# Attention and two mixtures of experts on one core: another order for the splits of k, v and q, and for six small operations of the routing

## The chip, the cores and the metric

One core of a Trainium2 chip runs the whole program in one launch. The metric is the device time of one launch in microseconds, the median of three runs: 1168.48 us (1166.46 to 1169.12). Profiles are of one execution each, which the hardware profiler records; their times are told beside their own execution's time.

## What is computed

```python
scores = scale * np.matmul(q, k.transpose(0, 1, 3, 2))          # 4 batches, 8 heads, 576 rows, 64 wide
scores = np.where(block_i >= block_j, scores, -1000000000.0)     # blocks of 64, causal by block
attn = np.exp(scores - np.max(scores, axis=-1, keepdims=True))
attn = attn / (np.sum(attn, axis=-1, keepdims=True) + 1e-09)
x = np.matmul(attn, v)                                           # heads joined: 2304 rows of 512
...
logits = xc @ w_gate                                             # rows with x @ w_skip > 0; expert = argmax of 8
gate_w = probs[np.arange(len(xc)), e_idx]
x[do_compute] = xc + gate_w * (np.maximum(xc @ w1[e], 0) @ w2[e])
...
out += p[:, e:e + 1] * (np.maximum(x @ w1[e], 0.0) @ w2[e])      # second mixture: all 4 experts, every row
```

Everything is float32 and is multiplied in pairs of a high part (a cast) and a low part (the rest), three products to a matmul.

## The kernel before

The program has three stages: attention with the routing (0 to about 224 us of the profile), the first mixture, and the second mixture, which is most of the time. The change lies in the first stage.

**Units.** Attention runs over 8 units of 4 heads (a batch, half its heads), numbered 0 to 7. Each unit has row tiles 0 to 4, in the order 0, 1, 3, 2, 4 (unit 7 in another): tile 0 has 64 rows and needs 64 columns of keys, tile rt has 128 rows and 64 + 128 rt columns. Tiles 2, 3 and 4 go as two items of two heads each, so a unit has 8 items. For each item TensorE (PE) writes scores `s` to PSUM (L285), VectorE (DVE) takes the row maxima `m` (L294), and ScalarE (ACT) writes the exponentials `E` (L301): 64 wide for tile 0, 192 for tile 1, 448 for tile 3, 320 for tile 2, 576 for tile 4. Then `E` is transposed to `eT`. Tiles 1 and 3 are transposed on PE (L327), and ACT and DVE write the high and low part (L329, L330). Tiles 0, 2 and 4 are split first: ACT casts `E` to the high half of `HL` (L333), GpSimd (POOL) subtracts (L334, 64x256, 128x640 and 128x1152 elements for the three tiles), and SyncE's queue (SP) starts a DMA that transposes (L335). PE multiplies `eT` with v into `og` (L359 to L361), and DVE divides (`r`, `x`, L367 to L370).

**Buffers of E.** `E` has four buffers (`EB = 4`), taken in turn. The fifth item of a unit, the first half of tile 2, takes the buffer of tile 0's item, so ACT's first `E` of 320 columns in a unit can't start until tile 0's split has read it, and the last to read it is POOL's subtraction of 64x256.

**The split of the next unit.** While a unit is scored, the parts of the next one are made by `split_unit`, a generator whose order a string sets: one letter is a step's work, a dot ends a step, and the attention loop runs two steps (`SN = 2`) for each group of scores. J scales k (ACT, L211); K casts it (ACT, `kh`, L212); k subtracts (POOL, `kl`, L213); V casts v (DVE, `vh`, L207) and v subtracts (POOL, `vl`, L208); A and B cast the two halves of q (ACT, `QH`, L230), a and b subtract (POOL, `QL`, L233); X and x copy pieces of q's parts for tile 4 (POOL, `q4h`, `q4l`, L222). Units 1 to 7 use `SO`, unit 0 `S0`.

**The routing.** When five or four tiles of x are done (two or one at the end), `route` picks each row's expert and its place in the sorted buffer `XS`: DVE makes one-hot rows `oh`, PE adds up ranks in the PSUM tile `pre` (L457 to L460), DVE sums the exponentials (L462 to L466) and multiplies `pre` by `oh` (L469), and POOL scatters the rows by indirect DMA (L478). `counts` (L491 to L502) follows the last batch.

The order on each engine is the order in which the Python code issues the work. Instructions of one engine run in that order.

Of the kernel before, what the change touches and what calls it, by code (L numbers as in the profile page):

```python
# [12 lines left out]
ALU = mybir.AluOpType  # L13
# [39 lines left out]
class Kernel:  # L53
# [49 lines left out]
    PW = 2  # L103
    PM = 1
    HV = ((7, 0),)
    SO = "J..K..V.k...A.v.B.a.b..X.x"

    def __init__(self, tc, q, k, v, wr, w11, w12, w21, w22, dp, out):
        self.tc, self.nc = tc, tc.nc
# [84 lines left out]
    def split_unit(self, u):  # L194

        nc = self.nc
        qr, kr, vr = self.raws.pop(u)
        QH = self.qk.tile([128, 2, S], F32R, name="QH")
        QL = self.qk.tile([128, 2, S], F32R, name="QL")
        KH, KL = self.kh[u % 2], self.kl[u % 2]  # L200
        vh, vl = self.vh[u % 3], self.vl[u % 3]
        self.units[u] = (QH, QL, KH, KL, vh, vl)
        V = nc.vector
        what = {
            "Q": lambda: nc.scalar.copy(QH, qr),
            "q": lambda: (V if self.QV else nc.gpsimd).tensor_tensor(QL, qr, QH.bitcast(F32), ALU.subtract),
            "V": lambda: V.tensor_copy(vh[:, :, :, 0:D], vr),  # L207
            "v": lambda: (V if self.VV else nc.gpsimd).tensor_tensor(vl, vr, vh[:, :, :, 0:D], ALU.subtract),  # L208
        }
        if u:  # L210
            what["J"] = lambda: nc.scalar.mul(kr, kr, 0.125)  # L211
            what["K"] = lambda: nc.scalar.copy(KH, kr)  # L212
            what["k"] = lambda: nc.gpsimd.tensor_tensor(KL, kr, KH.bitcast(F32), ALU.subtract)  # L213
        else:
            for x, y, i in (("0", "2", slice(0, 1)), ("1", "3", slice(1, 2))):
                what[x] = lambda i=i: V.tensor_scalar(KH[:, i], kr[:, i], 0.125, None, ALU.mult)
                what[y] = lambda i=i: V.scalar_tensor_tensor(KL[:, i], kr[:, i], 0.125, KH[:, i].bitcast(F32),
                                                             ALU.mult, ALU.subtract)
        def last(x):
            for a in range(2):  # L220
                p = slice(64 * a, 64 * a + 64)
                nc.gpsimd.tensor_copy(self.q4[u % 2][x][p].rearrange("p (c a) s -> p a c s", a=2)[:, a], (QH, QL)[x][p, :, S - 128:S])  # L222

        what["X"], what["x"] = lambda: last(0), lambda: last(1)
        for x in self.SO if u else self.S0:
            if x == ".":
                yield
            elif x in "AB":
                i = "AB".index(x)
                nc.scalar.copy(QH[:, i], qr[:, i])  # L230
            elif x in "ab":
                i = "ab".index(x)
                (V if i and not u else nc.gpsimd).tensor_tensor(QL[:, i], qr[:, i], QH[:, i].bitcast(F32), ALU.subtract)  # L233
            else:
                what[x]()
# [190 lines left out]
    def route(self, g, i0, i1):  # L426

        nc = self.nc
        n = i1 - i0
        yield from self.rest(self.RD)  # L430

        ts = []
        for x in range(i0, i1):
            i = (x + 4) % 5 if g == 3 else x
            ts.append((9 * (g // 2) + (5 * (g % 2) + i if i < 4 else 4), x - i0))
        lg = self.lgs[g][:, i0:i1]
        tl = lambda k, dt=F32: self.sm2.tile([128, 5, k], dt, tag=f"rt{k}{dt}", bufs=6, name="rt")[:, 0:n]
        mx, ex, cand, sm, ix, on = tl(1), tl(8), tl(8), tl(1), tl(1), tl(1)
        oh = tl(9, BF16)
        iota = self.iota[:, 0:n]  # L440
        nc.vector.tensor_reduce(mx[:, :, 0], lg[:, :, 0:8], axis=AX.X, op=ALU.max)
        nc.vector.tensor_tensor(ex, lg[:, :, 0:8], mx.to_broadcast([128, n, 8]), ALU.subtract)

        nc.vector.scalar_tensor_tensor(cand, ex, 0.0, iota, ALU.is_ge, ALU.mult)
        nc.vector.tensor_reduce(ix[:, :, 0], cand, axis=AX.X, op=ALU.min)
        nc.vector.tensor_tensor(cand, iota, ix.to_broadcast([128, n, 8]), ALU.is_equal)
        nc.vector.tensor_scalar(on, lg[:, :, 8:9], 0.0, None, ALU.is_gt)
        nc.vector.tensor_scalar(oh[:, :, 8:9], lg[:, :, 8:9], 0.0, None, ALU.is_le)
        nc.vector.tensor_tensor(oh[:, :, 0:8], cand, on.to_broadcast([128, n, 8]), ALU.mult)
        nc.scalar.activation(ex, ex, AF.Exp)  # L450
        yield
        yield from self.rest(self.PD)

        pre = self.pt([128, n, 9], "pre")
        for i in range(n):
            for j in range(i):
                nc.tensor.matmul(pre[:, i], lhsT=self.ones, rhs=oh[:, j], start=(j == 0), stop=False)  # L457
            nc.tensor.matmul(pre[:, i], lhsT=self.tri, rhs=oh[:, i], start=(i == 0), stop=False)
            nc.tensor.matmul(pre[:, i], lhsT=self.ones, rhs=self.hist, start=False, stop=False)
            nc.tensor.matmul(pre[:, i], lhsT=self.ones, rhs=self.base, start=False, stop=True)  # L460
        yield
        nc.vector.tensor_reduce(sm[:, :, 0], ex, axis=AX.X, op=ALU.add)  # L462
        nc.vector.tensor_scalar(sm, sm, 1e-9, None, ALU.add)
        for t, i in ts:
            x = self.x_of(t)
            nc.vector.reciprocal(x[:, DM + 1:RW], sm[:, i])  # L466
            nc.gpsimd.tensor_copy(x[:, DM:DM + 1].bitcast(I32), self.tok[:, t:t + 1])
        junk = tl(9)
        nc.vector.tensor_tensor(junk, pre, oh, ALU.mult)  # L469
        nc.vector.tensor_reduce(sm[:, :, 0], junk, axis=AX.X, op=ALU.add)  # L470
        sl = self.sm2.tile([128, 5], I32, tag="sl", bufs=5, name="sl")
        nc.vector.tensor_copy(sl[:, 0:n], sm[:, :, 0])
        for i in range(n):
            nc.vector.tensor_tensor(self.hist, self.hist, oh[:, i], ALU.add)
        for t, i in ts:
            while self.hold:
                yield
            ins = nc.gpsimd.indirect_dma_start(out=self.XS, out_offset=bass.IndirectOffsetOnAxis(ap=sl[:, i:i + 1], axis=0),  # L478
                                               in_=self.x_of(t), in_offset=None, bounds_check=E1 * N - 1,
                                               oob_is_err=False)  # L480

            for o in self.scat:
                self.tc.declare_no_dep(ins.ins, o.ins, reason="rows apart")
            self.scat.append(ins)
            for _ in range(self.XD):
                yield
# [744 lines left out]
```

## Time and profile before

| | |
|---|---|
| median of 3 runs | 1168.48 us (1166.46 to 1169.12) |
| profiled execution, its own time | 1173.74 us |
| span of its instructions | 1172.1 us, 1.6 us less than its time |
| granted clock of PE, mean of the span | 0.972 |
| PE busy | 1097.0 us (94%), 7197 matmuls |
| DVE, ACT, POOL busy | 760.6 us (65%), 518.0 us (44%), 574.1 us (49%) |

Busy shares over the whole span say little of the stage of the change: the second mixture, where PE is hardly ever idle, weighs most in them. The granted clock is in parts of full speed: 1.00 is 2.4 GHz, 0.50 is 1.2 GHz.

### The profile page before, as it was taken

To read this page: it belongs to the slowest core of one execution; us is meant where nothing else is said; L and a number is where in the kernel's file an instruction comes from. 1 tells how busy PE (TensorE), PEld (TensorE's weight loads), DVE (VectorE), ACT (ScalarE), POOL (GpSimd) and SP (SyncE) were. 2 spreads that over 40 slices of the span, in tenths; PEclk is the share of its full clock that TensorE was granted. 3 is DMA by queue.
4 is the path that set the end of the run, shared out by engine and by line. 5 is a ranking of instruction groups with operands and counts; after the bars stand their busy time and mean duration, and the time that the engine had idled before them with its cause. 6 is when DMAs were issued, how large, how long until landed. Compare 5 with 4: busy or idle time off the path is not lost.

```text
span 1172.1 us, 19018 instructions
## 1 busy us (share of the span) xinstructions
PE 1097.0 (94%) x7197; PEld 950.9 (81%) x7197; DVE 760.6 (65%) x1214; ACT 518.0 (44%) x852; POOL 574.1 (49%) x581
## 2 busy tenths in 40 slices
PE   5898978689999699999999999999999999999998
PEld 4788877567787589898899888999888888888886
DVE  6778776687528764666666666666846667676665
ACT  6988865366527544323232333233453333233331
POOL 6988883100111355454444454545665555555551
PEclk8999989699999799999999999999999999999999
DMA  5998849599614610111111111111321111111101
GB/s 194 217 226 200 179 118 253 170 323 388 235 46 158 218 55 20 53 37 40 52 36 36 38 36 54 36 37 54 128 71 54 54 54 55 55 54 55 36 1 72
DMA packets 119054, 123.04 MB, mean 105 GB/s; under 512 B 63341, under 2 KB 79725, under 8 KB 118928
## 3 DMA queue, kind: packets, MB, share of 16 engines
q1 hardware_dynamic: 116208, 116.82, 34.7%
q0 software_dynamic: 2720, 4.64, 1.1%
q8 instruction: 67, 1.10, 0.4%
q14 instruction: 59, 0.48, 0.1%
HBM read 91.83 MB, written 19.43 MB: 95 GB/s over the span
## 4 chain that ended last, share of the span: by engine, by line
PE 62%; DVE 3%; POOL 1%; ACT 1%; issue 1%; DMA 0%; SPq 0%; POOLq 0%
PE yp L672 11%; PE yp L671 11%; PE yp L673 11%; PE hp L672 9%; PE hp L673 9%; PE hp L671 9%; DVE xsl L875 1%; PE yp L732 0%; PE hp L713 0%; DVE acc L1005 0%; DVE xdl L865 0%; POOL C L943 0%; DVE C L943 0%; ACT hh L950 0%; DVE xs L871 0%
## 5 line engine op out<-in xcount | busy, mean ns | idle before, releaser
L1005 DVE SCALAR_TENSOR_TENSOR acc<-yp,p,acc 128x512 f32<-128x512 f32 x270 | 199.1, 747 | 109.3 <-PE yp L673 109.3
L950 ACT ACTIVATE hh<-C 128x512 fp32r<-128x512 f32 (+2 forms) x98 | 81.8, 834 | 349.2 <-DVE C L943 303.8
L671 PE MATMUL yp<-vh,hh 128*128 128x512 f32 x576 | 225.6, 392 | 2.8 <-ACT hh L950 2.4
L672 PE MATMUL yp<-vl,hh 128*128 128x512 f32 x576 | 226.3, 393 | 1.0 <-POOL vl L920 1.0
L673 PE MATMUL yp<-vh,hl 128*128 128x512 f32 x576 | 225.5, 391 | 0.3 <-DVE hl L951 0.3
L951 DVE SCALAR_TENSOR_TENSOR hl<-C,hh 128x512 fp32r<-128x512 f32 (+2 forms) x98 | 93.7, 957 | 99.6 <-ACT hh L950 99.6
L943 POOL TENSOR_TENSOR p<-C,p 128x256 f32<-128x256 f32 (+2 forms) x49 | 50.4, 1029 | 199.6 <-ACT p L940 199.6
L673 PEld LDWEIGHTS yp<-vh,hl 128*128 128x128 f32 x576 | 108.1, 188 | 24.7 <-DVE hl L951 1.6
L671 PEld LDWEIGHTS yp<-vh,hh 128*128 128x128 f32 x576 | 108.5, 188 | 20.9 <-ACT hh L950 2.9
L672 PEld LDWEIGHTS yp<-vl,hh 128*128 128x128 f32 x576 | 108.4, 188 | 18.5 <-POOL vl L920 1.8
L920 POOL TENSOR_TENSOR vl<-r,vh 128x512 fp32r<-128x512 f32 x64 | 83.4, 1315 | 78.4 <-ACT vh L917 78.4
L943 DVE TENSOR_TENSOR C<-hp,p 128x256 f32<-128x256 f32 (+2 forms) x147 | 80.2, 545 | 49.0 <-PE hp L673 24.2
L672 PE MATMUL hp<-xsl,th 128*128 128x256 f32 (+2 forms) x294 | 98.5, 335 | 1.2 <-DVE xsl L875 1.2
L671 PE MATMUL hp<-xsh,th 128*128 128x256 f32 (+2 forms) x294 | 98.4, 335 | 0.0
L673 PE MATMUL hp<-xsh,tl 128*128 128x256 f32 (+2 forms) x294 | 98.2, 334 | 0.0
L301 ACT ACTIVATE E<-s,m 128x320 f32<-128x320 f32 (+4 forms) x160 | 75.8, 531 | 14.2 <-DVE m L294 12.2
L741 POOL DMA_INDIRECT XN<-ys,xg x10 | 13.7, 1370 | 133.4 <-DVE ys L740 61.8
L943 POOL TENSOR_TENSOR C<-C 128x256 f32<-128x256 f32 (+2 forms) x49 | 52.7, 1076 | 45.6 <-ACT C L940 45.2
L294 DVE TENSOR_REDUCE m<-s 128x1 f32<-128x576 f32 (+3 forms) x80 | 64.7, 818 | 15.6 <-PE s L285 14.9
L334 POOL TENSOR_TENSOR HL<-E,HL 128x1152 bf16<-128x1152 f32 (+2 forms) x37 | 63.8, 1733 | 20.9 <-ACT HL L333 18.2
L671 PE MATMUL hp<-xdh,dh 128*128 128x256 f32 (+2 forms) x196 | 65.8, 336 | 1.2 <-ACT xdh L864 1.2
L672 PE MATMUL hp<-xdl,dh 128*128 128x256 f32 (+2 forms) x196 | 65.8, 336 | 0.2 <-DVE xdl L865 0.2
(220 smaller groups left out, 2780.6 us busy)
## 6 DMA issues: line engine op xcount, KB each, us to landing
r<-in_w_dram SPq DMA_DIRECT2D x128, 512.0 KB, 4.7
XN<-x SPq DMA_DIRECT2D x18, 256.0 KB, 2.3
vr<-in_v_dram SPq DMA_DIRECT2D x7, 640.0 KB, 7.8
xg<-XS SPq DMA_DIRECT2D x16, 257.0 KB, 10.0
out_dram<-acc SPq DMA_DIRECT2D x16, 256.0 KB, 2.0
qr<-in_q_dram SPq DMA_DIRECT2D x7, 576.0 KB, 4.8
kr<-in_k_dram SPq DMA_DIRECT2D x7, 576.0 KB, 6.1
x<-XN SPq DMA_DIRECT2D x12, 256.0 KB, 3.6
```

The source lines that it names most:

```text
L294: nc.vector.tensor_reduce(mo, mi, axis=ax, op=ALU.max, negate=True)
L301: nc.scalar.activation(e, views[j], AF.Exp, bias=m[:R, c:c + 1])
L334: (nc.vector if item[:2] in self.HV else nc.gpsimd).tensor_tensor(HL[:R, w:2 * w].bitcast(BF16), Et[:R, 0:w], HL[:R, 0:w], ALU.subtract)
L671: nc.tensor.matmul(out, lhsT=ah, rhs=bh, start=start, stop=False)
L672: nc.tensor.matmul(out, lhsT=ah, rhs=bl, start=False, stop=False)
L673: nc.tensor.matmul(out, lhsT=al, rhs=bh, start=False, stop=stop)
L741: nc.gpsimd.indirect_dma_start(out=self.XN, out_offset=bass.IndirectOffsetOnAxis(ap=xg[:, DM:DM + 1].bitcast(I32), axis=0), in_=ys, in_off ...
L920: nc.gpsimd.tensor_tensor(vl[:, f], r2[:, f], vh[:, f].bitcast(F32), ALU.subtract)
L943: add = lambda e, o, x, y: e.tensor_tensor(o, x, y, ALU.add)
L950: nc.scalar.activation(hh, C[:, i:i + 2], AF.Relu)
L951: V.scalar_tensor_tensor(hl, C[:, i:i + 2], 0.0, hh.bitcast(F32), ALU.max, ALU.subtract)
L1005: nc.vector.scalar_tensor_tensor(a, yp, self.p[:, n, e:e + 1], a, ALU.mult, ALU.add)
```

## The change

There are two parts. Counted in turns of the loop from a unit's first step, the string of units 2 to 7 had K in turn 1, V and k in turn 2, A and v in turn 4; now K and k stand in turn 1, V and v in turn 3, A alone in turn 4. J, B, a, b, X and x keep their turns. Unit 1 gets a string of its own, in which k follows K, and both halves of q precede v. In `route` the product with the ranks is issued ahead of the sum of the exponentials and of what follows from it.

```diff
-    SO = "J..K..V.k...A.v.B.a.b..X.x"
+    SO = "J..K.k...V.v.A..B.a.b..X.x"
+    S1 = "J.K.k...A.a.B.b.V.v.X.x"
...
-        for x in self.SO if u else self.S0:
+        for x in (self.S0, self.S1, self.SO)[min(u, 2)]:
...
         yield
+        junk = tl(9)
+        nc.vector.tensor_tensor(junk, pre, oh, ALU.mult)
         nc.vector.tensor_reduce(sm[:, :, 0], ex, axis=AX.X, op=ALU.add)
         nc.vector.tensor_scalar(sm, sm, 1e-9, None, ALU.add)
         for t, i in ts:
             x = self.x_of(t)
             nc.vector.reciprocal(x[:, DM + 1:RW], sm[:, i])
             nc.gpsimd.tensor_copy(x[:, DM:DM + 1].bitcast(I32), self.tok[:, t:t + 1])
-        junk = tl(9)
-        nc.vector.tensor_tensor(junk, pre, oh, ALU.mult)
         nc.vector.tensor_reduce(sm[:, :, 0], junk, axis=AX.X, op=ALU.add)
```

PE's and SP's instructions keep their order. In the changed kernel all lines from 107 on have a number that is higher by one (L334 is L335 there; inside `route` the reordered lines move as the diff shows). Three places:

POOL while unit 4 is scored and the first four tiles are scattered, before. `HL 64x256` is tile 0's split, `kl` the low part of k for unit 5.

```order
L334 TENSOR_TENSOR HL<-E,HL 128x1152
L467 COPY x<-tok 128x1 x4
L478 DMA XS<-x,sl 18432x514
L334 TENSOR_TENSOR HL<-E,HL 128x1152
L478 DMA XS<-x,sl 18432x514 x2
L334 TENSOR_TENSOR HL<-E,HL 64x256
L213 TENSOR_TENSOR kl_133<-kr,kh_132 128x1152
L478 DMA XS<-x,sl 18432x514
L208 TENSOR_TENSOR vl_164<-vr,vh_158 128x1280
```

And after the change:

```order
L335 TENSOR_TENSOR HL<-E,HL 128x1152
L470 COPY x<-tok 128x1 x4
L479 DMA XS<-x,sl 18432x514
L335 TENSOR_TENSOR HL<-E,HL 128x1152
L479 DMA XS<-x,sl 18432x514
L214 TENSOR_TENSOR kl_133<-kr,kh_132 128x1152
L479 DMA XS<-x,sl 18432x514
L335 TENSOR_TENSOR HL<-E,HL 64x256
L479 DMA XS<-x,sl 18432x514
L209 TENSOR_TENSOR vl_164<-vr,vh_158 128x1280
```

`kl` has moved from behind tile 0's split to ahead of it, and two scatters still precede the split. In the other units from 1 to 6 `kl` moves past that split in the same way.

POOL while unit 0 is scored and unit 1 is split, before (`vl_157`, `QL` and `q4` are unit 1's):

```order
L208 TENSOR_TENSOR vl_157<-vr,vh_151 128x1280
L334 TENSOR_TENSOR HL<-E,HL 128x640
L233 TENSOR_TENSOR QL<-qr,QH 128x576
L334 TENSOR_TENSOR HL<-E,HL 128x640
L233 TENSOR_TENSOR QL<-qr,QH 128x576
```

And after the change:

```order
L234 TENSOR_TENSOR QL<-qr,QH 128x576 x2
L335 TENSOR_TENSOR HL<-E,HL 128x640
L209 TENSOR_TENSOR vl_157<-vr,vh_151 128x1280
L223 COPY q4h_138<-QH 64x2x128 x2
L335 TENSOR_TENSOR HL<-E,HL 128x640
L223 COPY q4l_139<-QL 64x2x128 x2
L335 TENSOR_TENSOR HL<-E,HL 128x1152 x2
L214 TENSOR_TENSOR kl_131<-kr,kh_130 128x1152
L335 TENSOR_TENSOR HL<-E,HL 64x256
```

Both `QL` now stand ahead of the first 640 and `vl` behind it.

DVE while unit 6 is scored, before (`vh_151` is the cast of v for unit 7):

```order
L294 TENSOR_REDUCE m<-s 128x2
L207 CAST vh_151<-vr 128x20x64
L367 TENSOR_SCALAR r<-og 128x4
L368 RECIPROCAL r<-r 128x4
L370 TENSOR_TENSOR x<-og,r 128x256
L294 TENSOR_REDUCE m<-s 128x2
L330 TENSOR_TENSOR eT<-tp,eT 128x768
```

And after the change:

```order
L295 TENSOR_REDUCE m<-s 128x2
L368 TENSOR_SCALAR r<-og 128x4
L369 RECIPROCAL r<-r 128x4
L371 TENSOR_TENSOR x<-og,r 128x256
L295 TENSOR_REDUCE m<-s 128x2
L208 CAST vh_151<-vr 128x20x64
L331 TENSOR_TENSOR eT<-tp,eT 128x768
```

The cast of v goes behind the division and behind the maxima of the first 320 columns, in this unit and in units 1 to 5.

## Rows read from the trace of the kernel before

**Rows 1.** Stretches: us; busy us of PE, PEld, DVE, ACT, POOL; PEclk; DMA share; GB/s.
```profile
24.00:205.00 181.00, 154.54 (x2395) 144.23 (x2394) 129.30 (x286) 140.44 (x263) 139.69 (x119) 0.95 0.88 196
...
224.00:1172.00 948.00, 918.51 (x4586) 785.89 (x4586) 604.24 (x828) 357.05 (x549) 413.52 (x404) 0.98 0.26 85
```

**Rows 2.** PE's waits from 24 to 205 us: total, times, longest.
```profile
PE tp L327 <- ACT E L301: 8.6, 10, 3.4
...
PE s L285 <- POOL QL L233: 2.2, 1, 2.2
```

**Rows 3.** Timeline of POOL in unit 4: start, us, instruction, idle before.
```profile
103.53 1.40 POOL L478 DMA_INDIRECT XS<-x,sl  x1 [0.16 <-POOL HL L334]
105.23 0.97 POOL L478 DMA_INDIRECT XS<-x,sl  x1 [0.31 <-issue]
106.22 0.69 POOL L334 TENSOR_TENSOR HL<-E,HL 64x256 bf16<-64x256 f32 x1
106.85 2.64 POOL L213 TENSOR_TENSOR kl<-kr,kh 128x1152 fp32r<-128x1152 f32 x1
```

**Rows 4.** Timeline of ACT, units 3, 4 and 5.
```profile
78.75 1.17 ACT L212 CAST kh<-kr 128x1152 fp32r<-128x1152 f32 x1
...
82.94 0.96 ACT L301 ACTIVATE E<-s,m 128x320 f32<-128x320 f32 x2
...
101.76 1.17 ACT L212 CAST kh<-kr 128x1152 fp32r<-128x1152 f32 x1
...
106.95 0.95 ACT L301 ACTIVATE E<-s,m 128x320 f32<-128x320 f32 x2 [0.90 <-POOL HL L334]
...
123.89 1.17 ACT L212 CAST kh<-kr 128x1152 fp32r<-128x1152 f32 x1
...
128.47 0.99 ACT L301 ACTIVATE E<-s,m 128x320 f32<-128x320 f32 x2
```

**Rows 5.** Timeline of POOL, units 0 and 1.
```profile
22.12 2.53 POOL L208 TENSOR_TENSOR vl<-vr,vh 128x1280 bf16<-128x1280 f32 x1
...
33.62 5.94 POOL L334 TENSOR_TENSOR HL<-E,HL 128x1152 bf16<-128x1152 f32 x3
```

**Rows 6.** Timeline of ACT, unit 1.
```profile
32.77 0.91 ACT L301 ACTIVATE E<-s,m 64x64 f32<-64x64 f32 x4 [0.34 <-DVE m L294]
...
40.70 0.95 ACT L301 ACTIVATE E<-s,m 128x320 f32<-128x320 f32 x2
```

**Rows 7.** Timeline of POOL, unit 6.
```profile
150.00 1.01 POOL L478 DMA_INDIRECT XS<-x,sl  x1 [1.20 <-DVE hist L474]
151.04 0.69 POOL L334 TENSOR_TENSOR HL<-E,HL 64x256 bf16<-64x256 f32 x1
151.67 2.64 POOL L213 TENSOR_TENSOR kl<-kr,kh 128x1152 fp32r<-128x1152 f32 x1
```

**Rows 8.** Timeline of DVE, unit 6.
```profile
151.02 3.99 DVE L207 CAST vh<-vr 128x1280 f16<-128x1280 f32 x1
...
155.66 0.81 DVE L294 TENSOR_REDUCE m<-s 128x2 f32<-128x640 f32 x1
```

**Rows 9.** Timeline of ACT, unit 6.
```profile
148.13 1.16 ACT L212 CAST kh<-kr 128x1152 fp32r<-128x1152 f32 x1
...
156.57 0.95 ACT L301 ACTIVATE E<-s,m 128x320 f32<-128x320 f32 x2 [3.53 <-DVE m L294]
```

**Rows 10.** Busy time by stretch in units 1 and 6, columns as in the first group.
```profile
34.00:36.00 2.00, 2.00 (x14) 1.81 (x14) 1.44 (x5) 2.00 (x6) 2.00 (x2) 0.50 0.00 0
...
154.00:158.00 4.00, 0.56 (x4) 0.47 (x4) 3.93 (x7) 1.43 (x4) 3.52 (x4) 0.85 0.45 147
158.00:162.00 4.00, 4.00 (x47) 3.94 (x46) 1.70 (x5) 2.46 (x6) 3.81 (x3) 0.50 0.22 83
```

**Rows 11.** Timeline of DVE, the last batch of the routing.
```profile
219.28 0.15 DVE L462 TENSOR_REDUCE rt<-rt 128x1 f32<-128x8 f32 x1
...
219.73 0.15 DVE L469 TENSOR_TENSOR rt<-pre,rt 128x9 f32<-128x9 f32 x1
```

## The prediction

> **What bounds the kernel now.** I read the busy time by stretch first. From 24 to 205 us, the attention, PE is busy 154.5 of 181 us, ACT 140.4 and POOL 139.7 [rows 1]: three engines of nearly equal load that wait for each other, so no share tells which one a change must help. After 224 us PE is busy 918.5 of 948 us [rows 1]; the change touches nothing there, and what the attention gains or loses arrives at the end as a shift. I take it at full size.
>
> Then I read PE's waits in the attention. The largest is for ACT's exponentials, 8.6 us in ten waits, and unit 1's wait for the low part of q is 2.2 us [rows 2]. So ACT's exponentials pace the stage. On ACT I then looked for what holds them: in unit 4 the first E of 320 columns waited 0.90 us for POOL's HL [rows 4]. That is the buffer rule of the code at work, since this E takes the buffer that tile 0's split of 64x256 must have read, and that split ended at 106.22 + 0.69 = 106.91 us [rows 3], the E started at 106.95. Every unit has this E, it stands in ACT's one queue, and behind it come the next transposes and the next exponentials, so a delay of it delays the unit. The change puts kl (2.64 us [rows 3]) on POOL exactly ahead of that split. This is the centre of my forecast.
>
> **The change, part by part.** The new earliest start of that E is: kh cast by ACT and POOL free, then kl 2.64, then the split 0.69 us, together 3.33, with 0.04 us to the start of E as above.
>
> *Units 2, 3 and 5.* In unit 3 kh ends at 78.75 + 1.17 = 79.92 us, so E could start at 83.3; it started at 82.94 [rows 4]: **+0.4 us**. In unit 5 kh ends at 125.06, E could start at 128.4 and started at 128.47 [rows 4]: **0**, covered by the casts and exponentials that ACT does in between; were they shorter, the wait would show. Unit 2 has the same order without scatters; I take it like unit 5, between 0 and 0.4.
>
> *Unit 4.* Before, E already waited for the split, and the two scatters ahead of the split (1.40 and 0.97 us [rows 3]) stay ahead of it. kl comes in full: **+2.6 us**. Bounds: 0 if POOL, which is late here, lets ACT's delay be made up at the next 640 split, and 2.6 + 0.7 if the reordered small operations delay the first scatter by another split of 64x256.
>
> *Unit 1.* With its own string unit 1 has both QL ahead of the first 640 split and vl behind it; vl takes 2.53 us [rows 5], the two QL about as much, so POOL reaches the 1152 splits at the same time to within half a us. The three splits of one group start at 33.62 and end at 39.56 us [rows 5]; the third is tile 0's. With kl ahead of it, it ends between 41.7 (if it takes 0.69 us) and 42.2. E of 320 started at 40.70 [rows 6]. I take 41.9: **+1.2**, bounds +0.5 and +1.6. PE's stall of 2.2 us for QL [rows 2] does go, but I count it as nothing: during it ACT was idle only 0.34 us before the unit's first E [rows 6], and the E that POOL now holds back is later anyway.
>
> *Unit 6.* Here the change removes a wait. The cast of v took 3.99 us, from 151.02 to 155.01 [rows 8], and the maxima behind it, which E of 320 waited 3.53 us for [rows 9], started at 155.66. On POOL, split and kl ran back to back from 151.04 to 154.31 [rows 7], and the cast ended 0.70 us after kl. The cast was held up, not busy. The Trainium skill, SBUF — State Buffer, section "SBUF: two separate sides", says that VectorE and GpSimd share a port pair as an exclusive lock, and that the one which starts first has it while the other blocks. The trace agrees with the blocking, by the 0.70 us after kl; it does not agree with who is first, since the cast's record starts 0.02 us ahead of the split's, which was not lengthened. By the rule taken literally the cast should have run at once here, the 3.53 us of idle would have no cause, and the sum would be 2.0 us higher.
>
> Now the maxima of the 320 columns precede the cast, so that wait is gone. But E then meets the split: kh ends at 148.13 + 1.16 = 149.29 [rows 9], kl at 151.93, then come the token copies and one scatter of 1.01 us [rows 7], about 2 us with gaps, and the split to 154.6. E starts then instead of at 156.57 [rows 9]: **-2.0 us**. Bounds: 0 if the cast is held somewhere else, and -4.6 if PE's clock follows. PE, busy 0.56 of 4 us from 154, was granted 0.50 in the next 4 us, with 0.85 in the 4 before [rows 10], which is (0.5 x 4) + (0.15 x 4) = 2.6 us of full speed.
>
> *Routing.* In the last batch the sum began at 219.28 and the product at 219.73 us [rows 11]. The 0.45 us between filled the time until PE's ranks were there. Now they come behind the product, and everything that waits for the places (counts, last scatter, first load of the next stage) with them: **+0.4**, bounds 0 and +0.45. In earlier batches others' work hides it.
>
> Sum: 0.4 + 0 + 2.6 + 1.2 - 2.0 + 0.4 = **+2.6 us**. Against the profiled execution that is 1173.74 + 2.6 = 1176.3 us. That execution is 5.3 us above the median of the runs, 1168.48; moved over to it, the forecast is **1171.1 us**, +0.22%. About 0.2%, 2.3 us, is what a measurement of this kernel can tell from no change: below 1166.2 is faster, above 1170.8 slower. The forecast lies just beyond the line.
>
> **The rivals.** *PE sets the pace, faster.* If PE's own pauses count and not the held E, then the stall for QL pays 2.2 us, and the half clock after it (0.50 over 2 us from 34 [rows 10]) 1.0 more; unit 6 pays 2.0 and 2.6 of clock. Against that stand unit 4 with 2.6, unit 3 with 0.4 and the routing with 0.4. Sum -3.2 - 4.6 + 3.4 = -4.4, 1164.1 us. For it: PE's 154.5 us are the largest share. Against: ACT's 0.34 us of idle during the stall. It decides from the point where unit 1's E of 320 starts before 40.70 us.
>
> *Slower still.* Unit 4's E would wait 0.90 + 2.6 = 3.5 us, as long as unit 6's 3.53; if PE's clock drops there too, 2.6 us more. And the cast and split of unit 6 start 0.02 us apart, so in the timed runs the cast may have won the port and there is no 2.0 to gain. With the one or the other about +5: 1173.7 us, with both +7.2. The 5.3 us between profiled execution and median speak for it.
>
> *It hides.* ACT and POOL make up the late E by the next unit, and the gain of unit 6 covers the rest: 1168.5 us, within 1 us. Against it: ACT has one queue, and I found no idle of that size behind the E.
>
> **How the numbers follow.** Chances: forecast 0.40, with its own range 1168.9 to 1173; faster rival 0.27; slower still 0.20; hidden 0.13. Of the forecast's 0.40, 0.22 lie above 1170.8 and 0.18 within the line. So slower is 0.22 + 0.20 = 0.42, same 0.18 + 0.12 = 0.30, faster 0.27 + 0.01 = 0.28. The range reaches a little below the faster rival and above the slower one, 1163.5 to 1175.0; past it lie both extras of the slower rival and a bigger gain of clock.
>
> **What would show it.** Right: on ACT the first E of 320 columns waits for POOL's HL in units 1, 3, 4 and 6, in unit 4 for about 3.5 us; in unit 6 the cast of v takes about 1 us, and E starts 5.3 us after the end of kh instead of 7.3; PE's wait for QL in unit 1 is gone without the second unit starting sooner. Wrong: E of 320 in unit 4 comes 4.0 us after the end of kh there, as before (102.93 to 106.95 [rows 4]), where I expect 6.6, or the 64x256 split ends as early as it did; or the end of the attention moves by more than 3 us either way with these starts unmoved, in which case the clock or a transfer decided.

## The result and the profile after

The changed kernel takes 1177.65 us (median of 4 runs, 1175.32 to 1178.8), the kernel before beside it 1168.8 us (4 runs, 1166.46 to 1169.3): the ratio is 1.009, with a 95% interval of 1.0061 to 1.0119. It is slower by 8.9 us where 2.6 were forecast. The sign came out, the size lies outside the range. The ratio isn't the quotient of the two medians, which is 1.0076 here; over the runs below the two differ by up to 0.3%, so small differences between ratios should not be read closely.

The profiled execution of the change took 1177.47 us, close to its median. That of the kernel before lay 5.3 us above its own, so those two profiles differ by 3.7 us of span only. I therefore profiled the kernel before a second time (the run `again`, same code); its span is 1168.1 us. The part of the time in which the attention ends, up to the cast `cnt` of the counts, is compared below with both.

Busy time by stretch of the changed kernel, columns as in [rows 1]:

```profile
24.00:205.00 181.00, 155.07 (x2303) 144.19 (x2302) 129.84 (x276) 138.75 (x259) 135.58 (x112) 0.92 0.82 177
...
34.00:36.00 2.00, 1.07 (x18) 0.84 (x15) 1.26 (x2) 2.00 (x7) 1.86 (x4) 1.00 0.30 61
42.00:44.00 2.00, 0.25 (x4) 0.06 (x2) 1.39 (x2) 0.40 (x1) 2.00 (x3) 0.50 1.06 163
...
108.00:136.00 28.00, 24.92 (x329) 23.12 (x326) 17.89 (x31) 20.09 (x39) 22.76 (x17) 0.76 0.71 159
...
224.00:1172.00 948.00, 917.81 (x4590) 785.92 (x4590) 608.90 (x855) 360.86 (x554) 416.82 (x408) 0.98 0.26 85
```

After 224 us little has changed (917.81 against 918.51 us of PE [rows 1]). In the attention PE is about as busy as before, at a lower clock: 0.92 instead of 0.95 from 24 to 205 us, and 0.76 from 108 to 136 us, the time around unit 4.

PE's waits from 24 to 205 us in the changed kernel:

```profile
PE tp L328 <- ACT E L302: 11.3, 13, 2.5
PE s L286 <- ACT E L302: 6.4, 7, 3.2
```

The wait for unit 1's `QL` [rows 2] is gone, and from 34 to 36 us PE is granted 1.00 where it had 0.50 [rows 10]. The waits for ACT's E have grown instead, from 8.6 [rows 2] to 11.3 us at the transposes.

POOL of the changed kernel in units 1, 4 and 6 (timeline: start, us, instruction, idle before):

```profile
39.74 3.22 POOL L214 TENSOR_TENSOR kl<-kr,kh 128x1152 fp32r<-128x1152 f32 x1
42.91 0.66 POOL L335 TENSOR_TENSOR HL<-E,HL 64x256 bf16<-64x256 f32 x1
...
109.93 0.99 POOL L479 DMA_INDIRECT XS<-x,sl  x1 [0.17 <-POOL HL L335]
110.95 2.65 POOL L214 TENSOR_TENSOR kl<-kr,kh 128x1152 fp32r<-128x1152 f32 x1
113.76 1.39 POOL L479 DMA_INDIRECT XS<-x,sl  x1 [0.17 <-POOL kl L214]
115.17 0.69 POOL L335 TENSOR_TENSOR HL<-E,HL 64x256 bf16<-64x256 f32 x1
...
159.81 2.62 POOL L214 TENSOR_TENSOR kl<-kr,kh 128x1152 fp32r<-128x1152 f32 x1 [1.17 <-ACT kh L213]
...
164.22 0.68 POOL L335 TENSOR_TENSOR HL<-E,HL 64x256 bf16<-64x256 f32 x1
```

ACT of the changed kernel, the cast of k and the first E of 320 columns in units 1, 3, 4 and 6, and the cast of k in unit 5:

```profile
37.10 1.17 ACT L213 CAST kh<-kr 128x1152 fp32r<-128x1152 f32 x1
...
43.60 0.95 ACT L302 ACTIVATE E<-s,m 128x320 f32<-128x320 f32 x2 [1.94 <-POOL HL L335]
...
83.44 1.17 ACT L213 CAST kh<-kr 128x1152 fp32r<-128x1152 f32 x1
...
88.56 0.95 ACT L302 ACTIVATE E<-s,m 128x320 f32<-128x320 f32 x2 [0.81 <-POOL HL L335]
...
108.13 1.17 ACT L213 CAST kh<-kr 128x1152 fp32r<-128x1152 f32 x1
...
115.90 0.95 ACT L302 ACTIVATE E<-s,m 128x320 f32<-128x320 f32 x2 [2.83 <-DVE m L295]
...
135.46 1.17 ACT L213 CAST kh<-kr 128x1152 fp32r<-128x1152 f32 x1
...
158.57 1.16 ACT L213 CAST kh<-kr 128x1152 fp32r<-128x1152 f32 x1
...
165.75 0.97 ACT L302 ACTIVATE E<-s,m 128x320 f32<-128x320 f32 x2
```

In unit 1 `kl` and the split follow the 1152 splits [rows 5], and E starts 0.03 us after the split, at 43.60 instead of 40.70 us [rows 6]. In unit 6 `kl` now leads and the split starts 4.4 us after it, where the two ran in the other order [rows 7]. In unit 4 the rows answer to [rows 3, 4]: `kl` and a scatter now stand between the first scatter and the split, the split ends at 115.86, and E starts 0.04 us later. From the end of `kh` that is 115.90 - 109.30 = 6.60 us, where it was 4.02. (The row names DVE's maxima as the releaser, but these had ended at 111.78 us. This E takes tile 0's buffer, and its start follows the split by the same 0.04 us as before: POOL's split ended last.) The next unit's `kh` comes 27.33 us after this one's, where it was 22.13 [rows 4]: 5.20 us more, twice the hold.

DVE of the changed kernel in units 4 and 6 and in the last batch of the routing:

```profile
102.07 2.38 DVE L466 TENSOR_SCALAR rt<-rt 128x4 f32<-128x4 f32 x1
...
159.46 3.47 DVE L475 TENSOR_TENSOR hist<-hist,rt 128x9 bf16<-128x9 bf16 x5
...
165.31 0.82 DVE L208 CAST vh<-vr 128x1280 f16<-128x1280 f32 x1
...
225.42 0.17 DVE L464 TENSOR_TENSOR rt<-pre,rt 128x9 f32<-128x9 f32 x1 [0.34 <-PE pre L461]
```

In unit 6 the cast of v takes 0.82 us instead of 3.99 [rows 8], and E starts 165.75 - 159.73 = 6.02 us after the end of `kh` instead of 7.28 [rows 9]. It does not wait for POOL's split there: ACT had no idle just before it, and had lost 2.46 us earlier, at the second E of 448 columns, waiting for DVE. The first two rows show new holds, of which more below; the last answers to [rows 11].

The second profile of the kernel before, ACT in units 1, 4 and 5:

```profile
36.65 1.17 ACT L212 CAST kh<-kr 128x1152 fp32r<-128x1152 f32 x1
...
44.52 0.95 ACT L301 ACTIVATE E<-s,m 128x320 f32<-128x320 f32 x2 [3.01 <-DVE m L294]
...
62.60 1.16 ACT L212 CAST kh<-kr 128x1152 fp32r<-128x1152 f32 x1
...
107.68 1.17 ACT L212 CAST kh<-kr 128x1152 fp32r<-128x1152 f32 x1
...
112.88 0.95 ACT L301 ACTIVATE E<-s,m 128x320 f32<-128x320 f32 x2 [0.90 <-POOL HL L334]
...
129.81 1.17 ACT L212 CAST kh<-kr 128x1152 fp32r<-128x1152 f32 x1
```

and its busy time around unit 4, behind the held E of unit 6, and in the attention's last unit:

```profile
108.00:136.00 28.00, 24.34 (x375) 22.46 (x372) 19.95 (x38) 25.18 (x49) 26.82 (x20) 0.99 0.84 187
...
164.00:168.00 4.00, 4.00 (x53) 3.94 (x52) 1.72 (x5) 2.37 (x5) 3.81 (x3) 0.72 0.21 81
...
202.00:206.00 4.00, 3.94 (x83) 3.70 (x84) 0.92 (x5) 1.34 (x3) 1.73 (x4) 1.00 1.02 384
```

Unit 4 starts here at nearly the same time as in the changed kernel, and the same 28 us run at 0.99 instead of 0.76. From starts of `kh` (and of `cnt`, the end of the attention) like these, read in each trace, comes the table by which I followed the time, in us:

| | first `kh` | unit 1 to 2 | 2 to 3 | 3 to 4 | 4 to 5 | 5 to 6 | 6 to `cnt` | `cnt` | from `cnt` to the end |
|---|---|---|---|---|---|---|---|---|---|
| before | 35.84 | 20.81 | 22.10 | 23.01 | 22.13 | 24.24 | 72.49 | 220.62 | 951.5 |
| again (same code) | 36.65 | 25.95 | 22.10 | 22.98 | 22.13 | 24.25 | 65.08 | 219.14 | 949.0 |
| after | 37.10 | 23.80 | 22.54 | 24.69 | 27.33 | 23.11 | 68.22 | 226.79 | 949.0 |

After against again: the attention ends 7.65 us later and the span is 7.7 us longer, so all of it lies in the attention. The columns 2 to 3, 3 to 4 and 4 to 5 agree within 0.03 us between the two profiles of the kernel before, and there the change adds 0.44 + 1.7 + 5.20 = 7.3 us. The column 5 to 6 agrees between these two as well, but not beyond them: in both, PE's clock in that stretch was 0.93, and three kernels below in which unit 5 is unchanged (`s1_only`, `k_unit1`, `k_unit4`) show 22.65 to 22.67 us at 1.00. The changed kernel had 1.00 there too, so its 23.11 us are 0.45 more than like with like, and no gain. The columns unit 1 to 2 and 6 to `cnt` scatter by 5 and 7 us with the same code and can't be read from one profile.

### The profile page after: what moved, and what is told of

The parts are those of the page before. It is cut to its first block, busy times and chain, and to the rows that moved or that the text cites. A ratio compares the mean times of both kernels' runs of the same rounds, so it can differ in the third digit from the quotient of the medians.

```text
span 1175.8 us, 19027 instructions
## 1 busy us (share of the span) xinstructions
PE 1100.8 (94%) x7197; PEld 955.3 (81%) x7197; DVE 763.7 (65%) x1214; ACT 518.4 (44%) x852; POOL 574.7 (49%) x581
## 4 chain that ended last, share of the span: by engine, by line
PE 62%; DVE 3%; POOL 1%; ACT 1%; issue 1%; DMA 0%; SPq 0%; POOLq 0%
PE yp L673 11%; PE yp L672 11%; PE yp L674 11%; PE hp L673 9%; PE hp L674 9%; PE hp L672 9%; DVE xsl L876 1%; PE yp L733 0%; PE hp L714 0%; DVE acc L1006 0%; DVE xdl L866 0%; POOL C L944 0%; DVE C L944 0%; ACT hh L951 0%; DVE xs L872 0%
## 5 line engine op out<-in xcount | busy, mean ns | idle before, releaser
L944 DVE TENSOR_TENSOR C<-hp,p 128x256 f32<-128x256 f32 (+2 forms) x147 | 80.1, 545 | 49.0 <-PE hp L674 24.2
L335 POOL TENSOR_TENSOR HL<-E,HL 128x1152 bf16<-128x1152 f32 (+2 forms) x37 | 64.0, 1738 | 27.6 <-ACT HL L334 24.8
```

What stands on the lines that cost most here:

```text
L335: (nc.vector if item[:2] in self.HV else nc.gpsimd).tensor_tensor(HL[:R, w:2 * w].bitcast(BF16), Et[:R, 0:w], HL[:R, 0:w], ALU.subtract)
L944: add = lambda e, o, x, y: e.tensor_tensor(o, x, y, ALU.add)
```

## The experiments

Every kernel below is the kernel before with the edit shown, but for those with "after" in their label. Where strings differ by unit, the selector is the change's, `(self.S0, self.S1, self.SO)[min(u, 2)]`, or the one shown. The medians of the kernel before differ from one session on the chip to another (1166.66 to 1174.16 us), so only ratios are compared.

**Which part: k alone.**

```diff
-    SO = "J..K..V.k...A.v.B.a.b..X.x"
+    SO = "J..K.k.V....A.v.B.a.b..X.x"
+    S1 = "J..K..V.k...A.v.B.a.b..X.x"
```

> The string of units 2 to 7 has k in the step behind K as in the change; V, v and q stay where they were, unit 1 uses the old order of letters for everything, the routing is as before. Theory A (kl ahead of tile 0's split of 64x256 holds ACT's first E of 320 columns in every unit, and PE's clock falls after the longer holds): 4 to 9 us slower than before, that E waits for POOL's HL in at least three units, and in unit 4 it starts 6 us or more after kh ends. Rival B (the later cast of v meets kl on the shared port and DVE is late with the maxima): within 2 us of before, since the cast is not moved.

Measured: 1178.82 us, ratio 1.0092 (1.0059 to 1.0126). ACT of this kernel, unit 4 and the start of unit 5:

```profile
107.59 1.17 ACT L213 CAST kh<-kr 128x1152 fp32r<-128x1152 f32 x1
...
115.33 0.94 ACT L302 ACTIVATE E<-s,m 128x320 f32<-128x320 f32 x2 [3.46 <-POOL HL L335]
...
133.71 1.16 ACT L213 CAST kh<-kr 128x1152 fp32r<-128x1152 f32 x1
```

E waits 3.46 us for POOL's split, which is the forecast's "about 3.5", and the unit takes 26.12 us. Early `kl` alone is as slow as the whole change. (In unit 3 it also meets the cast of v, of which more under `k_eb5`.)

**v alone.**

```diff
-    SO = "J..K..V.k...A.v.B.a.b..X.x"
+    SO = "J..K...k.V.v.A..B.a.b..X.x"
+    S1 = "J..K..V.k...A.v.B.a.b..X.x"
```

> Only the cast of v and its subtraction are later, as in the change; k stays behind tile 0's split. Theory A: 0 to 5 us faster than before, the first E of 320 in unit 6 no longer waits 3.5 us for the maxima, since they stand ahead of the cast. Rival B: 4 to 9 us slower, the cast takes 1.5 to 2.6 us in units 2 to 6 as in the changed kernel and E of 320 waits for DVE's maxima.

Measured: 1172.78 us, ratio 1.0012 (0.9992 to 1.0032). The casts of v took 2.77, 2.47 and 2.41 us in units 2, 3 and 5 (1.84, 1.54 and 1.49 in the changed kernel) and 0.82 in unit 4 (2.59 there). Casts of v held up thus come without the 0.9%, and `k_only` has the 0.9% with the casts in their old place, though early `kl` holds one of them, in unit 3, for 3.19 us. In unit 6 E starts 3.73 us after the end of `kh` instead of 7.28, and the time does not fall. That alone doesn't settle the 2.0 us that I credited to unit 6, since here unit 4 takes 23.90 us instead of 22.13, at a clock of 0.93; `v7` below changes unit 6 only.

**Unit 1's string alone.**

```diff
     SO = "J..K..V.k...A.v.B.a.b..X.x"
+    S1 = "J.K.k...A.a.B.b.V.v.X.x"
```

> Only unit 1's string is new. Theory A: 0 to 3 us slower: the two early casts of q stand in ACT's queue and POOL reaches the splits of 1152 about 1.5 us later (35.1 instead of 33.6 us), although PE's wait of 2.2 us for QL is gone. Rival C (PE sets the pace): 2 to 4 us faster.

Measured: 1169.88 us, ratio 1.0027 (0.9998 to 1.0056). PE's stall for `QL` goes, and the string as a whole brings no gain. The cost, between nothing and 0.5%, is not settled further.

**The routing alone.**

```diff
+        junk = tl(9)
+        nc.vector.tensor_tensor(junk, pre, oh, ALU.mult)
         nc.vector.tensor_reduce(sm[:, :, 0], ex, axis=AX.X, op=ALU.add)
...
-        junk = tl(9)
-        nc.vector.tensor_tensor(junk, pre, oh, ALU.mult)
```

> Only the six operations of the routing are reordered. Theory A: within 2 us of before, at most 0.5 us later in the last batch. Rival D (the reordered scalar addition runs into POOL's split of 1152 in unit 4 and is held 2.4 us, the maxima behind it are late and PE's clock falls): 3 to 6 us slower, and that addition takes over 2 us in unit 4.

Measured: 1175.68 us, ratio 1.0036 (1.001 to 1.0062). DVE of this kernel, the batch in unit 4 and the last batch:

```profile
96.78 2.38 DVE L466 TENSOR_SCALAR rt<-rt 128x4 f32<-128x4 f32 x1
...
221.07 0.17 DVE L464 TENSOR_TENSOR rt<-pre,rt 128x9 f32<-128x9 f32 x1 [0.34 <-PE pre L461]
```

At the end the product waits for PE's ranks, 0.34 us here and 0.45 in the batch before, and from the batch's first maximum to `cnt` it is 2.92 us (219.51 to 222.43) instead of 2.57 (218.05 to 220.62), 0.35 more: close to the +0.4 of the forecast. But "in earlier batches others' work hides it" was wrong. In the first batch the small addition of 128x4, 0.17 us otherwise, now meets POOL's split of 128x1152 and takes 2.38 us; the interval from unit 3 to unit 4 is 23.77 us here, and 23.79 and 23.75 in two kernels below with this routing, where the old one has 22.96 to 23.01 (before, `again`, and `s1_only`, `v7` and `before_eb5`). Before, a cast of the places met that split, later and for 1.59 us. That is 0.8 us; what makes the timed ratio as high as 1.0036 the profile doesn't show.

**The new string of units 2 to 7 alone.**

```diff
-    SO = "J..K..V.k...A.v.B.a.b..X.x"
+    SO = "J..K.k...V.v.A..B.a.b..X.x"
+    S1 = "J..K..V.k...A.v.B.a.b..X.x"
```

> The string of units 2 to 7 as in the change, unit 1 and the routing as before. Theory A: as slow as the run with k alone or the changed kernel, 6 to 10 us over before. Rival (unit 1's string or the routing carries a good part by itself): under 5 us over before.

Measured: 1179.15 us, ratio 1.0088 (1.0062 to 1.0114). Unit 4 takes 26.24 us; its E starts 6.58 us after the end of `kh`. The string of units 2 to 7 carries the change's cost. Unit 1's string and the routing add nothing on top of it that these runs resolve, though the routing by itself showed 0.36%.

**The change with a fifth buffer of E.** Now the first E of 320 columns doesn't take tile 0's buffer.

```diff
-    EB = 4
+    EB = 5
```

> The changed kernel with a fifth buffer for E, so that the first E of 320 columns takes a buffer that tile 0's split does not read. Theory A (the hold of that E by kl ahead of the split is what makes the change slower): no wait of it for POOL's HL, E of 320 about 3.0 to 3.7 us after kh ends in units 1, 2, 3 and 5, and 5 to 9 us faster than the changed kernel, so within 3 us of before. Rival (the later order on POOL or DVE costs by itself, the buffer only passes it on): still 4 us or more slower than before.

Measured: 1172.61 us, ratio 1.0027 (1.0 to 1.0054). E starts 3.00 us after the end of `kh` in unit 4 and 3.01 in unit 1, though `kl` stands on POOL where it stood. The interval from unit 4 to unit 5 is 21.96 us instead of 27.33.

**The kernel before with a fifth buffer**, the same edit.

> The kernel before with a fifth buffer for E, the control of the run above. It frees unit 4's wait of 0.9 us and nothing else of that kind: theory A expects it 0 to 2 us faster than before, so that the fifth buffer alone does not explain a gain of 5 us in the run above. Rival: the fifth buffer is worth several us to either kernel, then 3 us or more faster.

Measured: 1169.18 us, ratio 0.9975 (0.9948 to 1.0003). The 0.90 us of unit 4 [rows 4] go too: its interval is 21.12 us.

**Early k alone with a fifth buffer**, `k_only` and this edit: does early `kl` cost anything but through the buffer?

> Early k alone (units 2 to 7) with five buffers of the exponentials instead of four. Theory, the held E of 320 columns: with a fifth buffer the E needs no split of tile 0, so it starts about 3.0 to 3.4 us after the end of kh in units 3 to 5, unit 4 goes back to an interval of kh to kh of 21 to 22 us (26.1 with four buffers), the end of the attention comes at 216 to 221 us, and the ratio is that of five buffers alone, 0.995 to 1.001, against 1.009 with four. Rival, early k costs by itself (its low part, its transposes or POOL's later queue): the ratio stays at 1.005 or more though E starts early.

Measured: 1170.33 us, ratio 0.9981 (0.9954 to 1.0009). ACT of this kernel, unit 4 and the start of unit 5:

```profile
109.85 1.17 ACT L213 CAST kh<-kr 128x1152 fp32r<-128x1152 f32 x1
...
114.02 0.96 ACT L302 ACTIVATE E<-s,m 128x320 f32<-128x320 f32 x2
...
131.72 1.17 ACT L213 CAST kh<-kr 128x1152 fp32r<-128x1152 f32 x1
```

and its busy time around unit 4:

```profile
104.00:128.00 24.00, 21.34 (x333) 19.59 (x332) 18.36 (x43) 20.52 (x39) 22.69 (x22) 1.00 0.77 183
```

E no longer waits in unit 4, PE's clock stays at 1.00, the unit takes 21.87 us instead of 26.12, and the ratio falls from 1.0092 to 0.9981. So in unit 4 early `kl` costs through the buffer and in no other way that shows.

In unit 3 an expectation missed, and it shows a second way. With five buffers as with four (`k_only`) E started 4.96 us after the end of `kh`, for want of its maxima (1.82 us of wait for DVE): the cast of v stands ahead of them, begins at 84.93 us, 0.18 after `kl`, and takes 3.14 us instead of 0.82, until 0.68 us after `kl`'s end. That is rival B's mechanism of the run `k_only`, although the cast was not moved. E is late by the same 1.94 us in both kernels. The interval from unit 3 to 4 is 24.91 us in `k_only`, 1.9 over before, with PE's clock at 1.00; here it is 26.34 instead of 22.96 (`before_eb5`), 3.4 over, with the clock at 0.94. The attention ended at 225.11 us in this profile, not by 221. The ratio, known to 0.3%, doesn't resolve these 3.4 us. The strings of the change put the cast behind the maxima and so avoid this: `so_only` has 23.91 us there.

**Is the rest in the strings or in the routing?** The change with five buffers stands at 1.0027, the kernel before with five at 0.9975. The strings alone with five buffers:

```diff
-    EB = 4
+    EB = 5
-    SO = "J..K..V.k...A.v.B.a.b..X.x"
+    SO = "J..K.k...V.v.A..B.a.b..X.x"
+    S1 = "J.K.k...A.a.B.b.V.v.X.x"
```

> Both new strings, the old routing, five buffers. If the 0.5% between the change and the kernel before, both with five buffers, lies in the routing, this one is at 0.995 to 1.000 and the interval from unit 3's kh to unit 4's is 22.0 to 23.0 us (23.8 with the new routing). If it lies in the strings (q ahead in unit 1, v late), it is at 1.001 to 1.004 like the change with five buffers.

Measured: 1169.13 us, ratio 0.9971 (0.9945 to 0.9997), and 22.98 us from unit 3 to unit 4. And `route_only` with the fifth buffer:

> The routing alone, five buffers. If the routing carries the 0.5%: 1.000 to 1.004, with the interval from unit 3's kh to unit 4's at 23.8 us, since the scalar addition is held 2.4 us by POOL's split. If the strings carry it: 0.995 to 0.999.

Measured: 1170.48 us, ratio 0.9982 (0.9953 to 1.0011), and 23.75 us from unit 3 to unit 4, with an addition of 2.37 us. The interval behaves as expected, but the times put the 0.5% in neither part: either half alone is about as fast as five buffers alone. The intervals of 1.0027 and 0.9975 nearly touch; whether the two halves cost something together only, or the 0.5% is scatter, stays open.

**The hold in one unit, unit 4.** Early `kl` only while unit 4 is scored, four buffers:

```diff
+    S1 = "J..K.k.V....A.v.B.a.b..X.x"
...
-        for x in self.SO if u else self.S0:
+        for x in (self.S0, self.SO, self.S1)[(u > 0) + (u == 5)]:
```

> Only the split of unit 5, made while unit 4 is scored, has kl ahead of tile 0's split; all else is as before. Theory A with a clock that follows: E of 320 in unit 4 comes 6.3 to 6.7 us after kh ends (4.0 before), PE's granted clock falls in the 12 us behind it, the next unit's kh is 4 to 6 us later than in the kernel before, and the time is 3 to 6 us over before. Rival (the hold of 2.6 us alone, no clock): the next unit's kh is 2.3 to 3 us later and the time 2 to 3 us over before.

Measured: 1170.59 us, ratio 1.0044 (1.0021 to 1.0066). ACT in units 4 and 5:

```profile
103.19 1.17 ACT L213 CAST kh<-kr 128x1152 fp32r<-128x1152 f32 x1
...
110.94 0.94 ACT L302 ACTIVATE E<-s,m 128x320 f32<-128x320 f32 x2 [3.46 <-POOL HL L335]
...
129.92 1.16 ACT L213 CAST kh<-kr 128x1152 fp32r<-128x1152 f32 x1
```

and the busy time behind the hold:

```profile
108.00:116.00 8.00, 4.24 (x47) 4.01 (x46) 2.50 (x5) 4.26 (x8) 7.61 (x6) 0.60 0.75 204
```

E comes 6.58 instead of 4.02 us after the end of `kh`, 2.56 late. The unit takes 26.73 instead of 22.13 us, 4.60 more. PE has little to do while E is held, and the clock granted to it falls to a mean of 0.60 of full speed over these 8 us. The other 2.0 us come behind the hold, at that clock. That they are the clock's is worked out from busy times: unit 4's stretch in the kernel before, then in this one, and unit 5's in the same two,

```profile
101.76:123.89 22.13, 19.49 (x307) 18.12 (x303) 15.57 (x30) 19.32 (x38) 21.21 (x17) 1.00 0.84 193
103.19:129.92 26.73, 21.54 (x307) 20.15 (x304) 15.59 (x30) 19.29 (x38) 22.45 (x17) 0.87 0.69 167
...
123.89:148.13 24.24, 21.82 (x339) 20.23 (x337) 17.43 (x40) 19.39 (x38) 19.00 (x14) 0.93 0.88 187
129.92:152.57 22.65, 20.26 (x339) 18.71 (x337) 17.17 (x40) 19.36 (x39) 17.73 (x14) 1.00 0.93 191
```

For the same 307 matmuls PE is busy 2.05 us longer, which is what the unit takes beyond the hold. In `k_only` and `so_only`, with the same hold, PE is busy 1.4 and 1.5 us longer, and the unit takes 3.99 and 4.11 us more. (In the changed kernel PE is busy 4.8 us longer there, of which 2.6 show in the unit's length.) In unit 5, which is the same code in both kernels and has no such hold, the lower clock is on the other side, and so are the 1.6 us. No run changes the clock alone. One held instruction in one unit is thus worth 0.44%, about 5 us of the timed runs, half of the change's cost.

**In one unit, unit 1**, the same with `(u == 2)`.

> Only the split of unit 2, made while unit 1 is scored, has kl ahead of tile 0's split. Theory A with a clock that follows: E of 320 in unit 1 starts 1 to 2.5 us later than at 40.7, PE's granted clock falls behind it, unit 2's kh is 2 to 4 us later and the time 1 to 4 us over before. Rival: the delay is made up by unit 2 and the time is as before.

Measured: 1169.47 us, ratio 1.0014 (0.9997 to 1.003). E started 5.18 us after the end of `kh` (3.69 in the first profile of the kernel before, but 6.70 in `again`; of eight profiles with unit 1 as before, six have 3.60 to 3.74 and two 6.70). Unit 1 takes 23.84 us, and unit 2, behind it, 25.25 instead of 22.10, at a clock of 0.86. The effect on the time is at the edge of what can be told.

**The kernel before again**, without an edit.

> The kernel before once more, with a profile of its own. Ratio 1.000 within its interval; the starts of E of 320 within 1 us of the first profile up to unit 6, with the cast of v held 4.0 us there. If the starts differ by several us, single profiles of two kernels can't be compared to a us.

Measured: 1168.09 us, ratio 0.9991 (0.9971 to 1.0011). DVE's cast of v in unit 1, in this profile:

```profile
39.04 3.92 DVE L207 CAST vh<-vr 128x1280 f16<-128x1280 f32 x1
```

and in the first profile of the kernel before:

```profile
37.69 1.36 DVE L207 CAST vh<-vr 128x1280 f16<-128x1280 f32 x1
```

The same instruction of the same code takes 1.36 us or 3.92 (it then ends 0.69 us after POOL's `kl`, which ran from 39.65 to 42.27 us), and unit 1 takes 20.81 or 25.95 us by it. In the last unit it is the other way round; busy time of the kernel before, first profile:

```profile
198.00:202.00 4.00, 1.52 (x32) 1.51 (x33) 0.77 (x3) 0.59 (x1) 1.35 (x4) 0.90 0.97 353
202.00:206.00 4.00, 4.00 (x40) 3.67 (x38) 0.77 (x3) 0.30 (x2) 0.00 (x0) 0.50 0.66 208
```

There PE ran little for 4 us and then at half clock, where `again` shows 1.00. `again` is 5.1 us longer in unit 1, 7.4 shorter from unit 6 to `cnt` and 2.5 shorter behind `cnt`; with 0.8 at the start that makes the 4.0 us by which its span is shorter. Of the 7.4 us 1.6 arise behind the held E of unit 6: the wait is 3.5 us in both, but in the 4 us that begin 1.5 us behind it `again` was granted 0.72 where the first profile shows 0.50 [rows 10].

**v late in unit 6 alone**, where its cast was held:

```diff
+    S1 = "J..K...k.V.v.A..B.a.b..X.x"
...
-        for x in self.SO if u else self.S0:
+        for x in (self.S0, self.SO, self.S1)[(u > 0) + (u == 7)]:
```

> Only unit 7's string has the later cast of v; everything else is as before. In all kernels with the old place the cast is held 3.98 to 3.99 us in unit 6 and E of 320 comes 7.2 to 7.3 us after kh. Theory A: there E comes about 3.7 us after kh as in the run with v alone, and the kernel is 1 to 4 us faster than before. Rival: what unit 6 gains is lost again by the end of the attention, within 1 us of before.

Measured: 1172.22 us, ratio 1.0019 (0.9987 to 1.0051). ACT in unit 6:

```profile
148.12 1.16 ACT L213 CAST kh<-kr 128x1152 fp32r<-128x1152 f32 x1
...
153.03 0.95 ACT L302 ACTIVATE E<-s,m 128x320 f32<-128x320 f32 x2
```

E starts 3.75 us after the end of `kh` instead of 7.28, and the kernel is no faster. The interval leaves room for a gain of 0.13%, 1.5 us, at most. Why a wait of 3.5 us on ACT goes for nothing stays open. From unit 6 to `cnt` eight profiles with the cast held show 65.08 to 74.79 us, the two without it (`v7` and the next kernel) 68.79 and 65.26; single profiles scatter too much there to tell.

**The best of both: a fifth buffer and v late in unit 6**, `v7` with `EB = 5`.

> The kernel before with a fifth buffer for E and with the later cast of v in unit 7's string alone: the two edits that take away a hold without adding one. Theory A: E of 320 about 3 us after kh in unit 4 and 3.7 us in unit 6, 2 to 6 us faster than before. Rival: what is gained by unit 6 is lost in the tail of the attention, within 1 us of before.

Measured: 1164.35 us, ratio 0.9977 (0.9959 to 0.9996), faster than both kernels. It gains 2.7 us, at the lower end of what was expected, and no more than the fifth buffer alone (0.9975).

## Why the prediction was right and wrong, point by point

- **The centre was right.** `kl` ahead of tile 0's split holds the first E of 320 columns. Its start in unit 4 was forecast 6.6 us after the end of `kh` and measured 6.60. `k_only` and `so_only` have the whole cost, and a fifth buffer takes it away: from early k (1.0092 to 0.9981), and from the change down to 1.0027. Of the signs named, the wait for tile 0's split came in units 1 to 5 and not in unit 6.
- **What failed is the price of that hold.** The sum took the hold alone, "+2.6 us" in unit 4, and left PE's clock to a rival. Unit 4 cost 5.20 us in the profile (27.33 - 22.13). `k_unit4` splits such a cost: 2.56 us of hold, 2.0 us behind it at a reduced clock, and other kernels with the same hold paid 3.99 and 4.11 us in the unit. The prediction had the figure, since it worked out 2.6 us of clock for unit 6 and named the same for unit 4 in "Slower still". A share of it should have stood in the sum, because E's wait in unit 4 was forecast as long as the one in unit 6 behind which the clock had fallen. The size isn't fixed by the length of the wait: behind the same wait in unit 6 `again` lost 1.6 us less.
- **Unit 6's -2.0 us failed too.** The wait of 3.53 us [rows 9] was real and went away, but v late in unit 6 alone brings at most 1.5 us and by its ratio nothing (1.0019), and late in all units nothing either (1.0012). Besides, E started 6.02 us after the end of `kh` where I forecast 5.3: `kl`, begun 0.08 us after the end of `kh` instead of 2.38 (151.67 - 149.29), now holds the small additions to `hist` for 3.47 us (0.98 in `again`), and the maxima behind them are late. With 2.6 more in unit 4 and nothing from unit 6, my own sum becomes 2.6 + 2.6 + 2.0 = 7.2 us. That is in size the rival with both extras, 1175.7 us, which I placed outside the range; its reason for unit 6, a cast that wins the port, did not come.
- **Units 2, 3 and 5** were put at 0, 0.4 and 0. E started 0.53, 0.93 and 0.54 us later than before after the end of `kh`, about 0.5 us above the forecast each: the split took 1.25 us where I reckoned with 0.69. Unit 3 to 4 shows 1.7 us more, of which 0.8 are the routing's. These are small misses of one sign.
- **Unit 1** was put at +1.2. E started 5.33 us after the end of `kh` instead of 3.69 (+1.6, the upper bound): `kl` took 3.22 us beside the cast of v instead of 2.64. POOL reached the 1152 splits at 35.07 us, 1.5 later than in [rows 5] and not within half a us. But `again` shows 6.70 us without the change, so one profile couldn't price this unit. That PE's stall for `QL` pays nothing fits `s1_only` (1.0027). PE did run at full clock from 34 to 36 us, where it had 0.50 [rows 10], and then stood at 42 us, at 0.50, with 0.25 of 2 us busy.
- **The routing's +0.4** was right at the end (0.35). The part said to be hidden cost 0.8 us in unit 4, where the shifted addition met POOL's split.
- **The base.** Taking the sum from the profiled execution to the median was right: the second profile of the same code has a span of 1168.1 us. But "the 5.3 us between profiled execution and median speak for" a cast that wins the port in unit 6 was wrong. In that unit the cast of v took 3.98 us in `again` as well; the two profiles differ by the clock behind it (1.6 us), in the last unit and behind `cnt`, and in unit 1 the other way.
- **The port.** The Trainium skill, SBUF — State Buffer, section "SBUF: two separate sides", says that a GpSimd operation and a VectorE operation with two SBUF inputs block each other too, where the former reads SBUF. The 3.47 us of `hist` agree, since both its inputs lie in SBUF and it ends 0.50 us after `kl`. I had used that section for the cast of v only, and had not asked which of DVE's small operations the moved `kl` would meet. The late cast of v in unit 4, 2.59 us from 111.71, was held by `kl` in the same way, and ended 0.70 us after it.

## What to carry to other kernels

Before an instruction is moved ahead in an in-order queue, look for what it overtakes, whose buffer that one frees, and who waits for the buffer; one more buffer is the cheap proof. Where the held instruction starves TensorE, charge the hold and the clock behind it: here 2.6 us of hold became 4.0 to 5.2 in the four kernels that have it. A wait that ends last in the trace isn't always worth its length: 3.5 us of it went here and no time was gained. And a single profile of a kernel whose engines race for a port can be 4 us off, so profile the unchanged kernel twice.

## What the runs showed that I had not expected

- An addition of 128x4 elements took 2.38 us instead of 0.17, and five additions of 128x9 took 3.47 instead of 0.98, each beside a long operation of GpSimd (the split of 128x1152 and `kl`). An operation of 0.17 us became fourteen times as long, and a change of GpSimd's order shifted which of VectorE's operations were hit.
- One and the same code showed a cast of 1.36 or of 3.92 us, and a first full unit of 20.8 or 25.9 us. The units from 2 to 5, between them, repeat to 0.03 us in these two profiles. Unit 5 to 6 took 24.2 or 22.7 us, of one code, at a clock of 0.93 or 1.00.
- A hold of 2.56 us in one of eight units, in a kernel of 1168 us, is worth 0.44% in timed runs (0.21 to 0.66%).
